# Attention on one Trainium2 core: one in three products for the row maxima is cut into pieces that fill a PSUM bank from both row halves

## The chip, the cores and the metric

The kernel runs on one core of one Trainium2 chip. The metric is the device time of one execution in microseconds (us). Before the change, three runs gave 2037.87, 2037.96 and 2039.02 us, with a median of 2037.96.

## The reference, cut to what matters

```python
def _A_ref(x, wqkv, wo):                      # B, S, D, H = 1, 2048, 640, 32
    qkv = (x @ wqkv).reshape(B, S, 3, H, Dh).transpose(2, 0, 3, 1, 4)
    q, k, v = qkv[0], qkv[1], qkv[2]          # Dh = 20
    scores = jnp.einsum("bhqd,bhkd->bhqk", q, k) * (Dh ** -0.5)
    p = _softmax(scores, axis=-1)
    o = jnp.einsum("bhqk,bhkd->bhqd", p, v)
    return o.transpose(0, 2, 1, 3).reshape(B, S, D) @ wo

def _B_ref(x, w_gate, w_up, w_down):          # F = 1728
    return (_silu(x @ w_gate) * (x @ w_up)) @ w_down

h = x + _A_ref(_layernorm(x), wqkv, wo)
h2 = h + _B_ref(_layernorm(h), w_gate, w_up, w_down)
```

The softmax needs the maximum of each row of scores. The kernel finds it in a first product of queries and keys, and computes the scores a second time, transposed, for the exponentials.

## The kernel before, in words

The program has three stages. The first, up to about 326 us, normalizes the tokens and makes queries, keys and values; a part of the row maxima is found there in the gaps (`max_four`, whose products have 256 columns, L211). The second, from 326 to about 1473 us, is the attention, and the change lies in it. The third is the feed-forward block.

The 32 heads are worked in 8 groups of 4, and the 2048 queries in 4 chunks of 512. A group and a chunk are a unit `u`; there are 32. A unit goes through 16 key tiles `kt` of 128 keys, which makes 512 key tiles in all. A head has only 20 numbers per token, so the matrices that are multiplied fill 60 or 62 rows of TensorE: two heads of a group lie in rows 0 to 63 and two in rows 64 to 127, and a product uses one of these two row halves (`b`, 0 or 1). Two products in different halves can run at the same time if they write to different PSUM banks.

In each key tile, TensorE has this to do, in the order that the string `ORDER` (L41) gives for even and odd tiles, `WsSmmSsM` and `WSsMMsSm`:

- `s` and `S` (`scores`, L1194): four score products of 512 columns, two in the first row half (`s`) and two in the second (`S`). ScalarE takes the exponential of each (L1200) into `probs`. The four write to four banks (`ps_one`) that go round, so each waits for the exponential of the tile before in the same place.
- `m` and `M` (`max_one`, L244): three products of 512 columns for the row maxima of a later unit, two in one half and one in the other, and in the next tile the other way round. VectorE reduces each to a maximum per row (L250). They use three banks (`ps_max`) that go round, so each waits for VectorE's reduction of the tile before in the same place. The two lists in `singles` hold 736 products each, 1472 in all, so they last for 490.7 key tiles.
- `W` (`weigh`, L1204): the probabilities of two tiles ago times the values. It is fp32, is done in two passes, and uses all 128 rows with four groups of 32 columns at a time. With `W` also go small steps: the end of a unit's maxima (`max_finish`), the copy of a finished output by ScalarE (`row_sums`, L1214), and preparation of the weights of the third stage by GpSimd.

When all maxima of a unit are there, `max_all` (L257) reduces the partial maxima, held in a tile `mx` per unit, over the four chunks of keys. The order of the instructions on each engine is the order of these calls; nothing is scheduled behind the author's back. An instruction that must wait for another engine waits in its engine's queue, in that order.

`clobber_nop` issues an empty instruction on VectorE, which only waits for semaphores and sets one. The first stage has 70 of them (L580): a product there is summed in one bank from both row halves, and the empty instruction stands between the halves so that they do not write to the bank at the same time.

Of the kernel before, what the change touches and what calls it, by code (L numbers as in the profile page):

```python
# [9 lines left out]
F32 = mybir.dt.float32  # L10
# [4 lines left out]
ALU = mybir.AluOpType  # L15
# [22 lines left out]
LOWEST = -3.4028234e38  # L38
GD = G * DH

ORDER = ("WsSmmSsM", "WSsMMsSm")  # L41


@with_exitstack
def tile_block(ctx: ExitStack, tc: tile.TileContext, x, wqkv, wo, wg, wu, wd, out):
# [123 lines left out]
            values[g][:, t0:t1], v_d[:, g].rearrange("(t p) w -> p t w", p=P)[:, t0:t1]  # L169
        )  # L170

    mxs = {u: stk.tile([P, 2, 2, TPC, NC], F32, name=f"mx{u}") for u in range(NU)}

    clock = dict.fromkeys(("PE", "ACT", "DVE", "POOL"), 0)
    held = [[0] for _ in range(5)]
# [64 lines left out]
    def max_one(u, kc, t, pair, b):  # L240

        ps = ps_max()
        rows = slice(b * ROW, b * ROW + NPART)
        nc.tensor.matmul(  # L244
            ps,
            queries[u][rows, pair, t * P : (t + 1) * P],
            keys[u // NC][rows, pair, kc * CH : (kc + 1) * CH],
            start=True, stop=True,
        )
        nc.vector.tensor_reduce(  # L250
            mxs[u][:, b, pair, t, kc : kc + 1], ps, axis=AX.X, op=ALU.max
        )

    def max_all(u):

        ends[u] = stk.tile([P, G * TPC], F32, name="neg", tag="neg", bufs=2)
        nc.vector.tensor_reduce(  # L257
            ends[u], mxs[u].rearrange("p b h t k -> p (b h t) k"), axis=AX.X, op=ALU.max, negate=True
        )

    def max_finish(u):
# [30 lines left out]
        if not in_projections(u, kc, t)  # L292
    ]


    evp_ctx = ExitStack()
    evp = evp_ctx.enter_context(tc.tile_pool(name="evp", bufs=2))
# [12 lines left out]
    with tc.tile_pool(name="pa", bufs=2) as pa:  # L310
# [442 lines left out]
        for c in range(NC):  # L753
            lns = []
            work = (some_keys + some_queries if c else first) + parts
            if c == NC - 1:
                work = some_keys + parts + some_queries

                es[:] = [e for e in es if e is not third]
                es.insert(1, z_tiles(NC)[0][:, :2])  # L760
            for j, (kind, *which) in enumerate(work):
                slot[0] = 18 * c + j
                while flips and not j:
                    flips.pop(0)()
                if c == 0 and j < 9:
                    for i in range(split_at[j], split_at[j + 1]):
                        split_w(i + 2)
                        if i % 2 == 1 and loaded < 8:
                            load_w(loaded)
                            loaded += 1  # L770
                if c + 1 < NC and j == 0:
                    es[:0] = [
                        t.rearrange("p k n -> p (k n)")[:, : 2 * EW].rearrange(
                            "p (i n) -> p i n", i=2
                        )
                        for t in z_tiles(c + 1)
                    ]
                    if c:
                        es[:] = es[2:] + es[:2]
                if c + 1 < NC and j == 10:  # L780
                    es[:] = [e for e in es if any(e is own for own in own_es)]
                if j == (0 if c else 3) and c + 1 < NC:
                    load_x(c + 1)
                    x_there[0] = clock["PE"] + X_LANDING
                    lns = norm(c + 1)
                if which:
                    if (c, j) == (0, 0):
                        first_blocks((0, 1), (1, 0), (1, 1), (0, 2), (1, 2))
                        for m, ps in enumerate(firsts):
                            keep(0, m, ps)  # L790
                    else:
                        (query_key if kind == "block" else value)(c, *which)
                else:
                    flip_ctx.close()
                    psum = ps_ctx.enter_context(
                        tc.tile_pool(name="psum", bufs=1, space=bass.MemoryType.PSUM)
                    )
                    turn, jobs = [0], [0]
# [51 lines left out]
    def ps_one():  # L850
# [3 lines left out]
            return psum_two.tile([P, CH], F32, name="ps_one", tag="ps_two")  # L854
        return psum.tile([P, CH], F32, name="ps_one", tag=f"ps_{(last + n - 1) % 3}")

    def ps_max():
        return psum.tile([P, CH], F32, name="ps_max", tag="ps_max", bufs=3)

    pp = att_ctx.enter_context(tc.tile_pool(name="pp", bufs=6, side="right"))  # L860
    evp_ctx.close()
# [382 lines left out]
            )  # L1244

    todo, tail, accs, closing, now = [], [], {}, {}, [0]
    singles = [[(*a, b) for a in rest] for b in range(2)]
    left = {u: sum(2 for a in rest if a[0] == u) for u in range(1, NU)}

    def next_max(b):  # L1250
        if singles[b]:
            a = singles[b].pop(0)
            max_one(*a)
            left[a[0]] -= 1
            if left[a[0]] == 0:
                max_all(a[0])
                closing[a[0]] = now[0] + 2

    def weigh_next():
        u, kt, probs = todo.pop(0)  # L1260
# [9 lines left out]
    for u in range(NU):  # L1270
# [4 lines left out]
        for kt in range(NT):  # L1275
# [626 lines left out]
```

## Time and profile before

| | |
|---|---|
| median of 3 runs | 2037.96 us |
| span of the profiled execution | 2036.6 us |
| attention with maxima, 326 to 1364 us | 1038 us |
| attention with maxima and the first output projections, 1364 to 1400 us | 36 us |
| rest of the attention, 1400 to 1473 us | 73 us |
| TensorE busy, share of the span | 99% |
| VectorE | 79% |
| ScalarE | 71% |

The profiled execution's own time is its span, from its first to its last instruction, 2036.6 us; the median of the runs is 1.4 us more. In the rows of the profile, PE is TensorE's products, PEld its weight loads, DVE VectorE, ACT ScalarE, POOL GpSimd. A row of the timeline gives the start and the length in us of one or several like instructions in a row, the line and operation, what is written and read, their number, and in brackets the idle time of the engine before. The names `ps_one` and `ps_max` tell scores and maxima apart.

### The profile page before, as it was taken

To read this page: it belongs to the slowest core of one execution; us is meant where nothing else is said; L and a number is where in the kernel's file an instruction comes from. 1 tells how busy PE (TensorE), PEld (TensorE's weight loads), DVE (VectorE), ACT (ScalarE), POOL (GpSimd) and SP (SyncE) were. 2 spreads that over 40 slices of the span, in tenths; PEclk is the share of its full clock that TensorE was granted. 3 is DMA by queue.
4 is the path that set the end of the run, shared out by engine and by line. 5 is a ranking of instruction groups with operands and counts; after the bars stand their busy time and mean duration, and the time that the engine had idled before them with its cause. 6 is when DMAs were issued, how large, how long until landed. Compare 5 with 4: busy or idle time off the path is not lost.

```text
span 2036.6 us, 40049 instructions
## 1 busy us (share of the span) xinstructions
PE 2012.6 (99%) x14322; PEld 1248.4 (61%) x14322; DVE 1608.8 (79%) x2826; ACT 1445.0 (71%) x2855; POOL 773.5 (38%) x1103
## 2 busy tenths in 40 slices
PE   8999999999999999999999999999999999999999
PEld 6999995333334333333333333345598888888888
DVE  5687778888888888888888888886378666676677
ACT  4677778999999999999999999987633222211221
POOL 6464423334342434352400011011146454754555
PEclk9999999999999999999999999999999999999999
DMA  7887563352634534435513131321158654974542
GB/s 238 262 254 261 167 206 88 115 159 80 187 104 122 168 113 146 147 129 176 156 46 79 27 92 47 92 62 55 34 182 303 221 192 157 345 273 159 202 150 94
DMA packets 194062, 310.01 MB, mean 152 GB/s; under 512 B 47760, under 2 KB 82576, under 8 KB 192840
## 3 DMA queue, kind: packets, MB, share of 16 engines
q1 hardware_dynamic: 187272, 283.85, 43.1%
q0 software_dynamic: 6496, 23.60, 3.9%
q8 instruction: 114, 1.87, 0.4%
q14 instruction: 84, 0.69, 0.1%
q10 hardware_dynamic: 96, 0.00, 0.0%
HBM read 207.75 MB, written 98.83 MB: 151 GB/s over the span
## 4 chain that ended last, share of the span: by engine, by line
PE 89%; DMA 3%; DVE 1%; ACT 1%; issue 0%; SPq 0%; POOL 0%; ACTq 0%; DVEq 0%; POOLq 0%
PE acc L1204 24%; PE ps_one L1194 16%; PE ps_a L1365 15%; PE ps_max L244 12%; PE ps_b L1459 8%; PE ps_one L575 7%; PE ps_max L211 3%; PE ps_max L925 2%; PE ps_b L925 1%; DMA halves<-j_d 1%; DMA k_stk<-k_d 0%; DMA q_stk<-q_d 0%; DMA units<-w_d 0%; ACT o L1214 0%; PE ps_max L960 0%
## 5 line engine op out<-in xcount | busy, mean ns | idle before, releaser
L1200 ACT ACTIVATE probs<-ps_one 128x512 f32<-128x512 f32 x2048 | 1056.7, 615 | 62.5 <-PE ps_one L1194 37.5
L250 DVE TENSOR_REDUCE mx<-ps_max 128x1 f32<-128x512 f32 x1472 | 926.1, 684 | 108.1 <-PE ps_one L1194 78.7
L1194 PE MATMUL ps_one<-q_stk,k_stk 62*128 62x512 f32 x2048 | 586.5, 451 | 2.7 <-DVE m L89 1.8
L1204 PE MATMUL acc<-probs,v_stk 128*32 128x512 f32 x4096 | 545.3, 605 | 0.7 <-ACT o L1214 0.6
L1194 PEld LDWEIGHTS ps_one<-q_stk,k_stk 62*128 62x128 f32 x2048 | 251.7, 184 | 433.1 <-ACT probs L1200 398.3
L244 PE MATMUL ps_max<-k_stk,q_stk 60*128 60x512 f32 x1472 | 381.4, 425 | 0.0
L244 PEld LDWEIGHTS ps_max<-k_stk,q_stk 60*128 60x128 f32 x1472 | 271.8, 186 | 23.6 <-DVE mx L250 0.9
L1580 DVE TENSOR_TENSOR tmp<-ps_a,tmp 128x512 f32<-128x512 f32 x208 | 141.2, 689 | 120.5 <-PE ps_a L1365 94.7
L233 DVE TENSOR_REDUCE mx<-ps_max 128x2 f32<-128x512 f32 x288 | 180.5, 685 | 63.6 <-PE ps_max L211 59.7
L1239 POOL TENSOR_TENSOR o<-o,rb 128x512 f32<-128x512 f32 x31 | 39.9, 1286 | 413.2 <-DMA q_stk<-q_d 235.8
L1204 PEld LDWEIGHTS acc<-probs,v_stk 128*32 128x32 f32 x4096 | 80.8, 108 | 175.6 <-issue 166.3
L223 ACT ACTIVATE ps_max<-ps_max 128x512 f32<-128x512 f32 x288 | 151.7, 584 | 46.3 <-PE ps_max L211 43.7
L1459 PE MATMUL ps_b<-halves,yp 128*128 128x320 f32 x1032 | 179.3, 309 | 1.9 <-DMA halves<-j_d 1.2
L1459 PEld LDWEIGHTS ps_b<-halves,yp 128*128 128x128 f32 x1032 | 165.2, 188 | 18.5 <-POOL yp L89 1.5
L1365 PE MATMUL ps_a<-t,units 128*128 128x512 f32 x624 | 162.6, 396 | 0.0
L1365 PE MATMUL ps_a<-z,units 128*128 128x512 f32 x516 | 133.9, 394 | 0.0
L89 POOL TENSOR_TENSOR yp<-y,yp 128x256 fp32r<-128x256 f32 x96 | 60.2, 627 | 188.3 <-ACT yp L88 180.3
L1365 PEld LDWEIGHTS ps_a<-t,units 128*128 128x128 f32 x624 | 112.6, 188 | 18.7 <-ACT tmp L1593 0.2
L1464 DVE TENSOR_TENSOR h<-ps_b,h 128x320 f32<-128x320 f32 x248 | 110.0, 481 | 6.8 <-PE ps_b L1459 5.3
L575 PE MATMUL ps_one<-z_hi,w_lo 64*128 64x512 f32 x380 | 112.6, 393 | 0.0
L575 PE MATMUL ps_one<-z_hi,w_hi 64*128 64x512 f32 x380 | 111.7, 393 | 0.0
L575 PE MATMUL ps_one<-z_lo,w_hi 64*128 64x512 f32 x380 | 111.2, 392 | 0.0
(211 smaller groups left out, 2640.3 us busy)
## 6 DMA issues: line engine op xcount, KB each, us to landing
units<-w_d SPq DMA_DIRECT2D x186, 256.0 KB
w_d<-stage SPq DMA_DIRECT2D x106, 256.0 KB
halves<-j_d SPq DMA_DIRECT2D x70, 320.0 KB
j_d<-stage SPq DMA_DIRECT2D x42, 320.0 KB
k_stk<-k_d SPq DMA_DIRECT2D x64, 160.0 KB
q_stk<-q_d SPq DMA_DIRECT2D x64, 160.0 KB
raw<-k_d SPq DMA_DIRECT2D x62, 160.0 KB
raw<-q_d SPq DMA_DIRECT2D x54, 160.0 KB
```

The lines of the kernel that those rows point to most:

```text
L223: nc.scalar.activation(ps, ps, AF.Relu)
L233: nc.vector.tensor_reduce(mx[:, b, :, t, kc], ps.rearrange("p (j n) -> p j n", j=2), axis=AX.X, op=ALU.max,)
L244: nc.tensor.matmul(ps, queries[u][rows, pair, t * P : (t + 1) * P], keys[u // NC][rows, pair, kc * CH : (kc + 1) * CH], start=True, stop=True,
L250: nc.vector.tensor_reduce(mxs[u][:, b, pair, t, kc : kc + 1], ps, axis=AX.X, op=ALU.max)
L575: nc.tensor.matmul(ps, a[rows], b[rows], start=(i == n == 0), stop=(i == 1 and n == last), skip_group_check=True,)
L1194: nc.tensor.matmul(ps, keys[u // NC][rows, p, kt * P : (kt + 1) * P], queries[u][rows, p, :], start=True, stop=True,)
L1200: nc.scalar.activation(probs[p][:, b, :], ps, AF.Exp, scale=scale)
L1204: nc.tensor.matmul(acc[32 * j : 32 * j + 32, :], values[u // NC][:, kt, j * VW : j * VW + 32], probs[j // 2][:, j % 2, :], start=(kt == 0) ...
L1365: nc.tensor.matmul(ps.rearrange("p (t n) -> p t n", t=TPC), w[k][:, i], z[k][:, :, j], start=(first and m == 0), stop=(last and m == len(n ...
L1459: nc.tensor.matmul(ps, a, b, start=(n == 0), stop=(n == len(pairs) - 1))
L1464: nc.vector.tensor_tensor(out=h, in0=ps, in1=h, op=ALU.add)
L1580: add = lambda out, ps, x: nc.vector.tensor_tensor(out=out, in0=ps, in1=x, op=ALU.add)
```

## The change

One in three of the products that were left for the attention stage (246 of 736 items of `rest`, each an item for both row halves) is done in another way. An item used to be two products of 512 columns, one in each row half, into two banks. Now it is two shared products: each takes 256 of the 512 key columns and has two pieces of 256 columns, the first from row half 0 into the left half of a bank (`x`), the second from row half 1 into the right half of the same bank (`X`). One reduction reads the whole bank and gives two maxima per row. Between the pieces stands an empty instruction on VectorE (`n`), which waits for the first piece; the second piece waits for it. Each key tile starts with `x` and has `X` as the last but one.

The order of a tile is now `WxnSmSsMXs` for all tiles: half 0 has `x`, `m` and two scores, half 1 has two scores, `M` and `X`. A tile still has three reductions. The 490 other items give 980 products of 512 columns, two in a tile; the 492 shared ones go one to a tile.

The three banks for maxima are now named one by one, and a counter (`place`) goes round over them; it is moved by one more at the start of each tile. So `x` of a tile takes the bank of the `m` of the tile before, `m` that of `M`, and `M` that of `X`.

The maxima of a unit get up to two places more (`EXTRA`). They are no longer kept in a tile per unit but in `found`, three buffers that go round; it is set up when a unit's first maximum comes, with a memset of the two extra places, and for 16 of 31 units with a copy of the maxima found in the first stage. `max_all` reduces over six places instead of four. In the first stage only the names of banks and the size of the tiles `mx` differ.

```diff
-ORDER = ("WsSmmSsM", "WSsMMsSm")
+ORDER = "WxnSmSsMXs"
+EXTRA = 2
+EVERY = 3
...
     def max_one(u, kc, t, pair, b):
...
         nc.vector.tensor_reduce(
-            mxs[u][:, b, pair, t, kc : kc + 1], ps, axis=AX.X, op=ALU.max
+            found_of(u)[:, b, pair, t, kc : kc + 1], ps, axis=AX.X, op=ALU.max
         )
+
+    found = {}
+
+    def found_of(u):
+
+        if u not in found:
+            f = found[u] = pp.tile([P, 2, 2, TPC, NC + EXTRA], F32, name="found", tag="found", bufs=3)
+            nc.vector.memset(f[:, :, :, :, NC:], LOWEST)
+            if u in mxs:
+                nc.vector.tensor_copy(f[:, :, :, :, :2], mxs.pop(u))
+        return found[u]
+
+    def max_start(u, kc, t, pair, half, column):
+
+        ps = ps_max()
+
+        def part(b):
+            rows = slice(b * ROW, b * ROW + NPART)
+            first = kc * CH + half * CH // 2
+            nc.tensor.matmul(
+                ps[:, b * CH // 2 : (b + 1) * CH // 2],
+                queries[u][rows, pair, t * P : (t + 1) * P],
+                keys[u // NC][rows, pair, first : first + CH // 2],
+                start=(b == 0), stop=True, skip_group_check=True,
+            )
+
+        def last():
+            part(1)
+            nc.vector.tensor_reduce(
+                found_of(u)[:, :, pair, t, column], ps.rearrange("p (b n) -> p b n", b=2),
+                axis=AX.X, op=ALU.max,
+            )
+
+        part(0)
+        return lambda: nc.vector.clobber_nop([nc.vector.lower_ap(ps)]), last
...
+    place = [0]
+
     def ps_max():
-        return psum.tile([P, CH], F32, name="ps_max", tag="ps_max", bufs=3)
+        place[0] += 1
+        return psum.tile([P, CH], F32, name="ps_max", tag=f"ps_max{place[0] % 3}")
...
-            order = ORDER[now[0] % 2] if singles[0] or singles[1] else "sSsSW"
+            order = ORDER if singles[0] or singles[1] or shared else "sSsSW"
+            place[0] += 1
             for op in order:
                 if op in "mM":
                     next_max(int(op == "M"))
+                elif op in "xX":
+                    next_shared(int(op == "X"))
+                elif op == "n":
+                    if begun:
+                        begun[0][1]()
```

TensorE's instructions of one key tile before the change, in their order in the program, with the engine that each waits for. `ps_one` are the scores, `ps_max` the maxima, `acc` is `W`:

```order
L1194 MATMUL ps_one_6348<-q_stk_2820,k_stk0_123 128x512 [waits Activation_49]
L1194 MATMUL ps_one_6351<-q_stk_2820,k_stk0_123 128x512 [waits Activation_49]
L244 MATMUL ps_max_6354<-k_stk0_123,q_stk_5786 128x512 [waits DVE_49]
L244 MATMUL ps_max_6357<-k_stk0_123,q_stk_5786 128x512 [waits DVE_49]
L1194 MATMUL ps_one_6360<-q_stk_2820,k_stk0_123 128x512 [waits Activation_49]
L1194 MATMUL ps_one_6363<-q_stk_2820,k_stk0_123 128x512 [waits Activation_49]
L244 MATMUL ps_max_6366<-k_stk0_123,q_stk_5786 128x512 [waits DVE_49]
L1204 MATMUL acc_6114<-probs_6303,v_stk0_124 32x512 x2
L1204 MATMUL acc_6114<-probs_6304,v_stk0_124 32x512 x2
```

The same of the changed program. `ps_max_8319` is the shared bank; its second piece waits for VectorE's sequencer, which is the empty instruction:

```order
L278 MATMUL ps_max_8319<-k_stk1_5587,q_stk_7396 128x256 [waits DVE_49]
L1250 MATMUL ps_one_8322<-q_stk_6848,k_stk1_5587 128x512 [waits Activation_49]
L250 MATMUL ps_max_8325<-k_stk1_5587,q_stk_7396 128x512 [waits DVE_49]
L1250 MATMUL ps_one_8328<-q_stk_6848,k_stk1_5587 128x512 [waits Activation_49]
L1250 MATMUL ps_one_8331<-q_stk_6848,k_stk1_5587 128x512 [waits Activation_49]
L250 MATMUL ps_max_8334<-k_stk1_5587,q_stk_7396 128x512 [waits DVE_49]
L278 MATMUL ps_max_8319<-k_stk1_5587,q_stk_7396 128x256 [waits DVE_sequencer_49]
L1250 MATMUL ps_one_8339<-q_stk_6848,k_stk1_5587 128x512 [waits Activation_49]
L1260 MATMUL acc_8311<-probs_8271,v_stk1_5588 32x512 x2
L1260 MATMUL acc_8311<-probs_8272,v_stk1_5588 32x512 x2
```

One 512-column product for maxima has become two pieces, the first at the head of the tile and the second ahead of its last score; behind `M` and its wait for VectorE, the second piece and a score are queued.

VectorE's instructions before the change around a change of unit (`mx14` is the unit's tile; L89 belongs to `max_finish`):

```order
L250 TENSOR_REDUCE mx14_139<-ps_max_11667 128x1 [waits PE_49]
L250 TENSOR_REDUCE mx14_139<-ps_max_11676 128x1 [waits PE_49]
L89 TENSOR_TENSOR m2_11694<-ps_one_11692,m2_11694 16x128 [waits DMAHW6_49,DMAHW5_49,DMAHW7_49,DMAHW0_49,Activation_49]
L250 TENSOR_REDUCE mx14_139<-ps_max_11710 128x1 [waits PE_49]
L250 TENSOR_REDUCE mx14_139<-ps_max_11713 128x1 [waits PE_49]
```

And after, where a unit's `found` is set up (the reduction of L287 is that of a shared bank; the empty instruction is not listed, its waits stand at the instruction behind it):

```order
L287 TENSOR_REDUCE found_11314<-ps_max_11650 128x2 [waits DVE_sequencer_49,PE_49]
L1281 RECIPROCAL r_11551<-r_11551 128x16 [waits DMAHW6_49,DMAHW7_49,DMAHW1_49,DMAHW0_49]
L266 MEMSET found_11696 128x16x2 [waits PE_49,DVE_sequencer_49]
L268 COPY found_11696<-mx13_133 128x16x2
L256 TENSOR_REDUCE found_11696<-ps_max_11694 128x1 [waits PE_49]
L256 TENSOR_REDUCE found_11696<-ps_max_11706 128x1 [waits PE_49]
L287 TENSOR_REDUCE found_11314<-ps_max_11688 128x2 [waits DVE_sequencer_49,PE_49]
L298 TENSOR_REDUCE neg_11711<-found_11314 128x16 [waits DVE_49]
```

The memset and the copy stand behind the empty instruction and ahead of the reduction of `m`.

More of the change, by code (lines that the diff above doesn't have):

```diff
@@ L170, in load_values @@
         )
-    mxs = {u: stk.tile([P, 2, 2, TPC, NC], F32, name=f"mx{u}") for u in range(NU)}
+    mxs = {
+        u: stk.tile([P, 2, 2, TPC, 2 if u else NC], F32, name=f"mx{u}")
+        for u in range(NU)
+        if u % NC < 2 or u == 2
+    }
     clock = dict.fromkeys(("PE", "ACT", "DVE", "POOL"), 0)
@@ L257, in max_all @@
         nc.vector.tensor_reduce(
-            ends[u], mxs[u].rearrange("p b h t k -> p (b h t) k"), axis=AX.X, op=ALU.max, negate=True
+            ends[u], (found.pop(u) if u else mxs[u]).rearrange("p b h t k -> p (b h t) k"), axis=AX.X, op=ALU.max, negate=True
         )
@@ L293, in tile_block @@
     ]
+    plain_items, shared = [], []
+    used = {}
+    for n, (u, kc, t, pair) in enumerate(rest):
+        if n % EVERY:
+            plain_items.append((u, kc, t, pair))
+        else:
+            extra = NC + used.setdefault((u, t, pair), 0)
+            used[u, t, pair] += 1
+            shared += [(u, kc, t, pair, 0, kc), (u, kc, t, pair, 1, extra)]
+    assert max(used.values()) <= EXTRA
     evp_ctx = ExitStack()
@@ L797, in tile_block @@
                     )
-                    turn, jobs = [0], [0]
+                    turn, jobs, three = [0], [0], [0]
                     def ps_one():
@@ L808, in ps_max @@
                             return psum_two.tile([P, CH], F32, name="ps_max", tag="ps_two")
-                        return psum.tile([P, CH], F32, name="ps_max", tag="ps_max", bufs=3)
+                        three[0] += 1
+                        return psum.tile([P, CH], F32, name="ps_max", tag=f"ps_max{three[0] % 3}")
                 if c == 0 and j == 6:
@@ L855, in ps_one @@
         return psum.tile([P, CH], F32, name="ps_one", tag=f"ps_{(last + n - 1) % 3}")
+    place = [0]
     def ps_max():
-        return psum.tile([P, CH], F32, name="ps_max", tag="ps_max", bufs=3)
+        place[0] += 1
+        return psum.tile([P, CH], F32, name="ps_max", tag=f"ps_max{place[0] % 3}")
     pp = att_ctx.enter_context(tc.tile_pool(name="pp", bufs=6, side="right"))
@@ L1246, in tile_block, with counted @@
     todo, tail, accs, closing, now = [], [], {}, {}, [0]
-    singles = [[(*a, b) for a in rest] for b in range(2)]
+    singles = [[(*a, b) for a in plain_items] for b in range(2)]
+    begun = []
     left = {u: sum(2 for a in rest if a[0] == u) for u in range(1, NU)}
+    def counted(u):
+        left[u] -= 1
+        if left[u] == 0:
+            max_all(u)
+            closing[u] = now[0] + 2
     def next_max(b):
@@ L1253, in next_max, with next_shared @@
             max_one(*a)
[L1254 to L1257, printed above, removed]
+            counted(a[0])
+    def next_shared(b):
+        if b == 0 and shared:
+            a = shared.pop(0)
+            begun.append((a[0], *max_start(*a)))
+        elif b == 1 and begun:
+            u, _, last = begun.pop()
+            last()
+            counted(u)
     def weigh_next():
```

## The prediction

> **What bounds the kernel now.** First I read the page's busy times and its chain of work that ended last:
>
> ```profile
> PE 2012.6 (99%) x14322; PEld 1248.4 (61%) x14322; DVE 1608.8 (79%) x2826; ACT 1445.0 (71%) x2855; POOL 773.5 (38%) x1103
> PE 89%; DMA 3%; DVE 1%; ACT 1%; issue 0%; SPq 0%; POOL 0%; ACTq 0%; DVEq 0%; POOLq 0%
> ```
>
> TensorE is never idle for long and 89% of the chain is its own. But the busy share is that of either row half, so it doesn't say how full the halves are. The stage that changes is the attention; the table of stretches and the groups within it:
>
> ```profile
> 326.00:1364.00 1038.00, 1035.59 (x7222) 409.97 (x7221) 921.25 (x1525) 1006.00 (x1982) 297.37 (x462) 1.00 0.37 111
> ...
> L1200 ACT ACTIVATE probs<-ps_one 128x512 f32<-128x512 f32 x1916 | 988.3, 614 | 31.0 <-PE ps_one L1194 6.1
> L250 DVE TENSOR_REDUCE mx<-ps_max 128x1 f32<-128x512 f32 x1436 | 903.8, 684 | 106.7 <-PE ps_one L1194 78.7 <-PE ps_max L244 24.0
> L89 DVE TENSOR_TENSOR m<-ps_one,m 16x128 fp32r<-16x128 f32 x30 | 8.4, 279 | 7.8 <-ACT m L88 7.0
> L1214 ACT ACTIVATE o<-acc 128x512 f32<-128x512 f32 x29 | 18.3, 631 | 0.7 <-DMA o_d<-o 0.7
> L1225 DVE RECIPROCAL r<-r 128x16 f32<-128x16 f32 x29 | 7.0, 243 | 0.0
> ```
>
> The 1916 exponentials are 479 key tiles in 1038.0 us, 2.17 us a tile, and the granted clock (1.00) leaves nothing to explain. ScalarE and VectorE are busy for 97% and 89% of it: little room. So one tile has to be read piece by piece. The timeline, with TensorE's, one weight load's and VectorE's rows:
>
> ```profile
> 801.82 1.89 DVE L250 TENSOR_REDUCE mx<-ps_max 128x1 f32<-128x512 f32 x3 [0.24 <-PE ps_one L1194]
> ...
> 803.16 0.50 PE L1194 MATMUL ps_one<-q_stk,k_stk 62*128 62x512 f32 x2
> 803.50 0.40 PE L244 MATMUL ps_max<-k_stk,q_stk 60*128 60x512 f32 x1
> 803.50 0.39 PE L1194 MATMUL ps_one<-q_stk,k_stk 62*128 62x512 f32 x1
> 803.74 0.52 PE L244 MATMUL ps_max<-k_stk,q_stk 60*128 60x512 f32 x2
> 803.76 0.18 PEld L244 LDWEIGHTS ps_max<-k_stk,q_stk 60*128 60x128 f32 x1
> 803.94 1.89 DVE L250 TENSOR_REDUCE mx<-ps_max 128x1 f32<-128x512 f32 x3 [0.23 <-PE ps_max L244]
> 803.97 0.40 PE L1194 MATMUL ps_one<-q_stk,k_stk 62*128 62x512 f32 x1
> 804.30 1.06 PE L1204 MATMUL acc<-probs,v_stk 128*32 128x512 f32 x8
> 805.30 0.50 PE L1194 MATMUL ps_one<-q_stk,k_stk 62*128 62x512 f32 x2
> ```
>
> One half does score 803.16, maximum 803.50, maximum 803.74, score 803.97; the other score 803.16, score 803.50, maximum 803.76, and then nothing until `W` at 804.30. So the fuller half sets the tile: 0.34 (the first product waits for its weights) + 0.24 + 0.23 + 0.33 (the last one, until `W`) + 1.00 (`W`) = 2.14 us. A 512-column product takes 0.235 of its half. The emptier half's maximum is held up by something else: VectorE's three reductions begin at 801.82 and end 1.89 later, at 803.71, and its weight load follows 0.05 after, at 803.76. That wait is hidden here, since the half has a product less to do.
>
> ScalarE in the same tile:
>
> ```profile
> 803.70 2.07 ACT L1200 ACTIVATE probs<-ps_one 128x512 f32<-128x512 f32 x4
> ```
>
> Four exponentials take 2.07 with the tail of the last; less one of 0.614, three spacings are 1.456, so ScalarE needs 0.485 each and 1.94 a tile. VectorE's spacing is (1.89 − 0.684)/2 = 0.603, so it needs 1.81 a tile.
>
> **The change part by part.** *The pieces.* How long 256 columns take shows in the first stage, where both halves run two such products each and then go on with 512 columns:
>
> ```profile
> 300.11 0.46 PE L211 MATMUL ps_max<-raw,raw 60*128 60x256 f32 x4
> 300.35 0.40 PE L575 MATMUL ps_one<-z_hi,w_lo 64*128 64x512 f32 x1
> ```
>
> Two more rows of that stage, the reductions with two outputs and the empty instructions (least, median and greatest duration in ns):
>
> ```profile
> L233 DVE TENSOR_REDUCE mx<-ps_max x288: 645/683/695, 50.0 to 321.3; 128x2 f32<-128x512 f32 x144
> L580 DVEq EVENT_SEMAPHORE  x70: 21/542/2474, 27.0 to 316.2; - x70
> ```
>
> A half runs two of them in 0.24 (300.11 to 300.35), so a piece costs 0.12, half of a whole product, and both weight loads hide. The Trainium skill ("TensorEngine Tiling (Array Packing)", Instruction Overhead) gives each matmul some 60 cycles beyond its columns. By that rule a piece would be (256+60)/(512+60) of 0.235, an estimate of 0.13, and the gain below 2 to 5 us smaller; the rows show no such cost.
>
> Each half now has three products and a piece. TensorE's own path is `x`, `m`, two scores: 0.34 − 0.115 = 0.225 until `m`, 0.235, 0.235, 0.33, and `W` 1.00: 2.025. That is 0.115 less than 2.14, the most that the change can give.
>
> *The wait that is uncovered.* `M` takes the bank of the tile before's `X`, which is reduced last, and now has `X` behind it in the same half. From the stamp of one tile's first product: `m` at 0.225; its reduction 0.44 later (803.50 to 803.94) at 0.665; the third reduction ends 1.89 later at 2.555 (a reduction with two outputs takes 683 ns by L233's row, like the others); `M`'s weight load at 2.605; its data 0.11 later at 2.715, as it must wait for these weights (the first product of a tile loses the same: 0.34 against 0.235). `X` follows at 2.95, is through 0.12 later, `W` 0.10 after that (0.33 − 0.235) at 3.17, and the next tile but one begins 1.00 later at 4.17. Two tiles in 4.17 are 2.085 a tile. This is longer than TensorE's 2.025, so VectorE's chain becomes the bound, and of the 0.115 only 2.14 − 2.085 = 0.055 remains. Queued behind `M`'s wait are `X`, a score and `W`; the score isn't due before `M`'s wait is over, `X` and `W` are late.
>
> *ScalarE's chain.* First exponential 0.54 after the stamp (803.16 to 803.70), fourth done 2.07 later at 2.61; its bank goes to the last score of the next tile, 0.05 and 0.11 later at 2.77; 0.33 to `W`, 1.00: 4.10, or 2.05 a tile. It is hidden, by 0.035 only.
>
> *The empty instruction.* `x` has streamed at 0.225 and can be seen 0.205 later (0.44 − 0.235), at 0.43. The empty instruction takes 0.02 at least by L580's row, whose median of 0.54 holds its waiting. I take 0.05. At 0.48 it is out of the way; VectorE's next reduction is due at 0.665 and `X` far later. Cost nothing, covered by 0.185 of idle time of VectorE; beyond that each 0.1 of delay costs 0.05 a tile.
>
> *Per unit.* 31 memsets and 16 copies are not in the trace of before. The nearest rows are small VectorE instructions of 0.243 (L1225) and 0.279 (L89); the lower end is nothing. They stand behind the empty instruction, so the reduction due at 0.665 starts at 0.72 after a memset alone and 0.96 with a copy: 15 × 0.055 + 16 × 0.295 = 5.5 us if each delay goes through, 0 if the other tiles absorb it; I take 4. ScalarE's copies of the output (29 of 0.631) come on top of its 1.94; it had 0.20 a tile to catch up and now has 0.145, so it is late for longer. I take 0.15 each, 4 us, between 0 and 9. `max_all` over six places and the two sequencer waits lie in VectorE's gap. The first and third stages keep their instructions; the maxima still last for some 491 tiles.
>
> **The sum.** 490 × 0.055 = 27 us, less 4 and 4, makes 19. The profiled execution's span is 2036.6 and would be 2017.6; the median of the runs is 1.4 above the span, so **2019 us**. A measurement can tell about 0.2%, 4 us, from no change. With the ends of the unit costs (0 to 15) and 0.01 a tile on the chain either way (5 us), the likeliest case alone gives 2007 to 2031.
>
> **The rivals.**
>
> *Full balance, 1990 us.* If `M`'s bank came free 0.06 earlier in each tile, TensorE's 2.025 would hold: 490 × 0.115 = 56, less 8. For it: VectorE has 0.25 of idle time a tile. Against: the weight load that follows a reduction's end by 0.05 already in this trace.
>
> *No change, 2034 to 2042.* ScalarE's chain is only 0.035 below the bound. If an exponential slips by 0.04, four of them bring it to the old time. For it: its 97% in the stage. Against: the spacing of 0.485.
>
> *Products start in order, 2046 us.* If the halves kept the program's order, the last score could not start before `X`: 2.95 + 0.33 + 1.00 = 4.28, 2.14 a tile, no gain, and 8 for the units on top. The trace speaks against it: in the tile above the second score of the emptier half starts at 803.50, and a maximum that stands ahead of it at 803.74. The Trainium skill ("TensorE: Matmul & The Clock Gate", Part 3, The mechanism) says that matmuls start and end strictly in program order; the trace disagrees.
>
> *Slower, by the empty instruction, about 2094 us.* It stands in VectorE's queue ahead of the reduction of `m`. If it passed not 0.05 but 0.54 after `x` (L580's median), it would end at 0.97 and that reduction start 0.305 late; half of this a tile is 0.15, less the 0.055, 490 × 0.0975 = 48, and 8: 56 us slower. The point from which it decides is 0.25 later than I take it. For it: all of those 0.54 could be its own. Against: the 21 ns of the fastest.
>
> **How the numbers follow.** Forecast (2007 to 2031) 0.62; full balance 0.08; no change 0.10; in order 0.06; the empty instruction 0.14. Faster by over 0.2%: 0.62 + 0.08 = 0.70; same 0.10; slower 0.06 + 0.14 = 0.20. The range from 1998 to 2048 holds the forecast, no change and in order, and a part of neither end: 0.78, with what lies between the cases about 0.8.
>
> **What would show it.** Right: a tile of about 2.08 in the attention, in one length or alternating ones that average to it; `M`'s weight load 0.05 after the end of the third reduction in most tiles, and its product of 0.50 instead of 0.39; `W` following `X`; VectorE's idle time ahead of the first reduction still near 0.25. Wrong: a tile of 2.03 with `W` following a score (full balance); exponentials with no idle time and scores that wait for them (ScalarE); last scores that never start before `X` (in order); first reductions that begin right at the end of the empty instruction, later than 0.44 after `m` (the empty instruction). Unit changes longer by over half a microsecond each would make the sum's last two terms wrong.

## The result, and the profile after

The changed kernel takes 2023.57 us (median of 4 runs, 2022.97 to 2023.85); the kernel before, on the same chip, 2038.49 (4 runs, 2037.87 to 2041.11). The ratio is 0.9927, with an interval of 0.9913 to 0.9941: 14.9 us faster, where 19 were forecast. The spans of the profiled executions, 2036.6 and 2021.5, differ by 15.1. Counted from one first product of `W` to that of a later tile, the attention divides like this:

| | before | after |
|---|---|---|
| tiles 0 to 477 (maxima, no projections) | 1034.9 us | 1016.3 us |
| of them, tiles under 2.2 us: number and mean | 406 of 2.127 us | 408 of 2.066 us |
| the longer ones: what they are over that mean, together | 18.5 us | 28.8 us |
| tiles 478 to 489 (the last with maxima) | 47.4 us | 51.2 us |
| of them, the eight with output projections, 478 to 485 | 36.2 us | 38.8 us |
| and the four behind these, 486 to 489 | 11.2 us | 12.4 us |
| the 21 tiles after these, up to the last one | 62.4 us | 62.5 us |
| from there to the end | 565.6 us | 565.2 us |

So the common tile gives 478 × 0.0605 = 28.9 us; the longer tiles take 10.3 back and tiles 478 to 489 take 3.8, which leaves 14.8.

The page, busy times and chain:

```profile
PE 1994.3 (99%) x14814; PEld 1267.7 (63%) x14814; DVE 1608.1 (80%) x2873; ACT 1434.8 (71%) x2855; POOL 773.1 (38%) x1103
PE 85%; DMA 3%; DVE 2%; issue 2%; POOL 1%; ACT 1%; SPq 1%; ACTq 0%; DVEq 0%; POOLq 0%
```

TensorE's share of the chain went from 89 to 85% and VectorE's from 1 to 2%. The sums hardly tell what happened; a pair of tiles does. Most of TensorE's products, two of its weight loads, and VectorE's reductions, in the timeline (start, length, engine, line; ps_max at L278 are the pieces, at L250 the whole products for maxima):

```profile
812.21 0.68 DVE L287 TENSOR_REDUCE found<-ps_max 128x2 f32<-128x512 f32 x1
812.47 0.38 PE L278 MATMUL ps_max<-k_stk,q_stk 60*128 60x256 f32 x1
...
812.69 0.38 PE L250 MATMUL ps_max<-k_stk,q_stk 60*128 60x512 f32 x1
812.81 0.50 PE L1250 MATMUL ps_one<-q_stk,k_stk 62*128 62x512 f32 x2
812.94 0.18 PEld L250 LDWEIGHTS ps_max<-k_stk,q_stk 60*128 60x128 f32 x1
...
813.04 0.40 PE L250 MATMUL ps_max<-k_stk,q_stk 60*128 60x512 f32 x1
...
813.11 1.29 DVE L256 TENSOR_REDUCE found<-ps_max 128x1 f32<-128x512 f32 x2 [0.23 <-PE ps_max L250]
813.15 0.39 PE L1250 MATMUL ps_one<-q_stk,k_stk 62*128 62x512 f32 x1
813.28 0.28 PE L278 MATMUL ps_max<-k_stk,q_stk 60*128 60x256 f32 x1
...
813.49 1.07 PE L1260 MATMUL acc<-probs,v_stk 128*32 128x512 f32 x8
...
814.32 0.68 DVE L287 TENSOR_REDUCE found<-ps_max 128x2 f32<-128x512 f32 x1
814.48 0.38 PE L278 MATMUL ps_max<-k_stk,q_stk 60*128 60x256 f32 x1
...
815.05 0.18 PEld L250 LDWEIGHTS ps_max<-k_stk,q_stk 60*128 60x128 f32 x1 [0.16 <-DVE found L287]
815.06 0.49 PE L250 MATMUL ps_max<-k_stk,q_stk 60*128 60x512 f32 x1
...
815.18 0.43 PE L1250 MATMUL ps_one<-q_stk,k_stk 62*128 62x512 f32 x1
815.39 0.27 PE L278 MATMUL ps_max<-k_stk,q_stk 60*128 60x256 f32 x1
...
815.59 1.06 PE L1260 MATMUL acc<-probs,v_stk 128*32 128x512 f32 x8
...
816.59 0.38 PE L278 MATMUL ps_max<-k_stk,q_stk 60*128 60x256 f32 x1
```

The first tile is 2.01 long (812.47 to 814.48), the second 2.11 (814.48 to 816.59). In both, the load of `M`'s weights waits for the shared reduction of the tile before. In the first this reduction ends at 812.89 and the load follows 0.05 after, at 812.94; that costs nothing, since the half is busy with a score until about 813.05 (812.81 + 0.235) and `M` starts at 813.04. In the second the reduction, begun at 814.32, ends at 815.00 and the load comes at 815.05, when the half has just come free; the data wait for the weights, the product shows 0.49 instead of 0.40, and `X` and `W` come after. In 382 of the 407 common tiles in which the trace shows this load, it follows the reduction's end by 0.05 to 0.07, as the prediction said it would in most; it holds up the product only in every second one. The predicted chain, step by step from the first stamp: reduction of `m` 0.665, measured 0.64; third reduction's end 2.555, measured 2.53; `M`'s load 2.605, measured 2.58; `W` 3.17, measured 3.12; the next tile but one 4.17, measured 4.12. How often this wait leaves the weight loads idle, in the waits of the stretch from 326 to 1340 us (total, times, longest):

```profile
PEld ps_max L250 <- DVE found L287: 33.0, 188, 0.3
```

188 waits of 0.18. The common tiles are of two kinds, 212 of 2.016 and 196 of 2.120 us, and in all 345 places where two common tiles follow each other there is one of each, as in the pair.

The empty instruction, with its form (least, median and greatest ns) and those who waited for it (total us, times):

```profile
L293 DVEq EVENT_SEMAPHORE  x492: 21/50/50, 322.6 to 1391.2; - x164
...
  PEld ps_max L278: 7.5, 15
  PE ps_max L278: 1.5, 5
```

It takes 50 ns. The last two rows are the weight loads and the products of the same pieces, so 15 of 492 second pieces waited for it, 7.5 us in all, and none of them in a common tile: seven (3.2 us) lie in tiles where the maxima of a unit are transposed at a change of group, and eight (4.2 us) in tiles 479 to 489, of which rows are shown under the experiments.

### The profile page after: what moved, and what is told of

Same layout as the page of the kernel before. It is cut to its first block, busy times and chain, and to the rows that moved or that the text cites. A ratio compares the mean times of both kernels' runs of the same rounds, so it can differ in the third digit from the quotient of the medians.

```text
span 2021.5 us, 42075 instructions
## 1 busy us (share of the span) xinstructions
PE 1994.3 (99%) x14814; PEld 1267.7 (63%) x14814; DVE 1608.1 (80%) x2873; ACT 1434.8 (71%) x2855; POOL 773.1 (38%) x1103
## 4 chain that ended last, share of the span: by engine, by line
PE 85%; DMA 3%; DVE 2%; issue 2%; POOL 1%; ACT 1%; SPq 1%; ACTq 0%; DVEq 0%; POOLq 0%
PE acc L1260 24%; PE ps_a L1440 15%; PE ps_one L1250 11%; PE ps_max L278 8%; PE ps_b L1534 8%; PE ps_one L627 7%; PE ps_max L250 6%; PE ps_max L217 3%; PE ps_max L981 2%; PE ps_b L981 1%; DMA halves<-j_d 1%; DVE found L256 0%; DMA w_d<-stage 0%; DMA r_d<-r 0%; PE ps_max L1016 0%
## 5 line engine op out<-in xcount | busy, mean ns | idle before, releaser
L256 DVE TENSOR_REDUCE found<-ps_max 128x1 f32<-128x512 f32 x980 | 630.5, 685 | 84.8 <-PE ps_max L250 59.8
L278 PEld LDWEIGHTS ps_max<-k_stk,q_stk 60*128 60x128 f32 x984 | 181.9, 185 | 393.8 <-DVE found L256 375.9
L250 PE MATMUL ps_max<-k_stk,q_stk 60*128 60x512 f32 x980 | 392.0, 419 | 0.2
L287 DVE TENSOR_REDUCE found<-ps_max 128x2 f32<-128x512 f32 x492 | 335.4, 682 | 1.3 <-PE ps_max L278 1.3
L278 PE MATMUL ps_max<-k_stk,q_stk 60*128 60x256 f32 x984 | 325.5, 331 | 3.2 <-DVEq L293 1.5
L1250 PEld LDWEIGHTS ps_one<-q_stk,k_stk 62*128 62x128 f32 x2048 | 303.8, 184 | 25.5 <-ACT probs L1256 20.4
L250 PEld LDWEIGHTS ps_max<-k_stk,q_stk 60*128 60x128 f32 x980 | 181.2, 185 | 49.2 <-DVE found L287 33.2
```

The costliest lines, as they stand in the source:

```text
L250: nc.tensor.matmul(ps, queries[u][rows, pair, t * P : (t + 1) * P], keys[u // NC][rows, pair, kc * CH : (kc + 1) * CH], start=True, stop=True,
L256: nc.vector.tensor_reduce(found_of(u)[:, b, pair, t, kc : kc + 1], ps, axis=AX.X, op=ALU.max)
L278: nc.tensor.matmul(ps[:, b * CH // 2 : (b + 1) * CH // 2], queries[u][rows, pair, t * P : (t + 1) * P], keys[u // NC][rows, pair, first : ...
L287: nc.vector.tensor_reduce(found_of(u)[:, :, pair, t, column], ps.rearrange("p (b n) -> p b n", b=2), axis=AX.X, op=ALU.max,)
L1250: nc.tensor.matmul(ps, keys[u // NC][rows, p, kt * P : (kt + 1) * P], queries[u][rows, p, :], start=True, stop=True,)
```

## The experiments

**Who sets the tile: reductions made shorter.** In three kernels only a part of a bank is reduced, so that maxima are missing, while TensorE's work stays.

In the kernel before (`light_before`):

```diff
-            mxs[u][:, b, pair, t, kc : kc + 1], ps, axis=AX.X, op=ALU.max
+            mxs[u][:, b, pair, t, kc : kc + 1], ps[:, : CH // 4], axis=AX.X, op=ALU.max
```

> The kernel before, but each reduction for the maxima reads only the first 128 of 512 columns (the maxima are then of a part of the keys). If the tile before was set by TensorE's fuller half, VectorE's shorter work changes nothing: 2.13 us a tile and 2033 to 2039 us in all. If VectorE's wait was part of the bound already, the tile falls by 0.05 or more and the time by 24 or more.

Measured: 2036.72 us, ratio 0.9991 (0.9982 to 1.0000), common tile 2.128. So VectorE did not set the tile before. Nor did ScalarE: the change leaves its exponentials as they were, and the tile fell below 2.127. TensorE's fuller half is left.

In the changed kernel (`light_after`), both kinds of reduction:

```diff
-            found_of(u)[:, b, pair, t, kc : kc + 1], ps, axis=AX.X, op=ALU.max
+            found_of(u)[:, b, pair, t, kc : kc + 1], ps[:, : CH // 4], axis=AX.X, op=ALU.max
...
-                found_of(u)[:, :, pair, t, column], ps.rearrange("p (b n) -> p b n", b=2),
+                found_of(u)[:, :, pair, t, column], ps.rearrange("p (b n) -> p b n", b=2)[:, :, : CH // 8],
```

> The changed kernel with reductions that read 128 columns of each bank (64 of each piece). VectorE's round of banks is then short. Theory that VectorE's round sets the changed tile (4.13 for two): what is left is TensorE's own path of 2.01 a tile, 478 x 0.055 = 26 us less than the change, about 1997. Rival that ScalarE's chain sets it: 2.05 a tile or more, 2015 to 2024. Rival that TensorE's own path is already what shows: no change, 2023.

Measured: 2008.04, ratio 0.9850 (0.9833 to 0.9866), common tile 2.040. That is between the two theories' numbers: the tile falls by 0.026 without VectorE's work, so VectorE did set it, and then stops short of 2.01. What stops it is in the timeline of this run. Each row of exponentials holds the two that touch a narrow window around the weight load of a tile's last score, which is the row behind it:

```profile
806.85 1.16 ACT L1256 ACTIVATE probs<-ps_one 128x512 f32<-128x512 f32 x2
807.52 0.18 PEld L1250 LDWEIGHTS ps_one<-q_stk,k_stk 62*128 62x128 f32 x1
...
808.86 1.22 ACT L1256 ACTIVATE probs<-ps_one 128x512 f32<-128x512 f32 x2
809.52 0.18 PEld L1250 LDWEIGHTS ps_one<-q_stk,k_stk 62*128 62x128 f32 x1
```

An exponential takes 0.614, as before the change, so the first of each two ends at 807.46 and 809.47; the loads follow 0.06 and 0.05 after. That is the chain by which the prediction gave ScalarE 2.05 a tile.

Only the shared reduction, to half of its columns (`half_read`):

```diff
-                found_of(u)[:, :, pair, t, column], ps.rearrange("p (b n) -> p b n", b=2),
+                found_of(u)[:, :, pair, t, column], ps.rearrange("p (b n) -> p b n", b=2)[:, :, : CH // 4],
```

> The changed kernel, where only the reduction of the shared bank reads less (128 of 256 columns of each piece). It is the last of a tile, and its end is what the next tile's M waits for. Theory of VectorE's round: its end comes some 0.25 sooner, two tiles would take 3.88, so TensorE's 2.01 to 2.02 is reached, about 1998 us. If VectorE's work as a whole were the bound, a third of the gain of the kernel with all reductions shortened. If ScalarE's chain is the bound: no change, 2020 to 2024.

Measured: 2011.87, ratio 0.9867 (0.9852 to 0.9881), common tile 2.042, again above the expected, for the same reason. But it has 0.024 of the 0.026 that `light_after` takes off the common tile, and 11.7 of its 15.5 us, where a third was expected if VectorE's total work were the bound: the end of the last reduction matters.

Both engines lightened (`light_both`): `light_after`, and exponentials of 448 of 512 columns with the rest set to 1, so that one in eight probabilities is not computed:

```diff
-        nc.scalar.activation(probs[p][:, b, :], ps, AF.Exp, scale=scale)
+        n = 7 * CH // 8
+        nc.scalar.activation(probs[p][:, b, :n], ps[:, :n], AF.Exp, scale=scale)
+        nc.vector.memset(probs[p][:, b, n:], 1.0)
```

> The changed kernel with VectorE's reductions cut to 128 columns, and with exponentials of 448 of 512 columns as well (VectorE sets the other 64 probabilities to 1). If the tile that is left when VectorE's work is short (2.04) is set by ScalarE's chain, from a tile's first score over four exponentials to the next tile's last score, it is now shorter by 4 x 0.06, and TensorE's own path is left: 2.01 a tile, 478 x 0.03 = 14 below the kernel with short reductions alone, about 1994 us. If something else sets the 2.04 (TensorE's queue, the empty instruction): no change, 2006 to 2010.

Measured: 1985.43, ratio 0.9735 (0.9716 to 0.9753), common tile 2.015; the longer tiles fell too, from 27.4 us over the mean in `light_after` to 19.5, which the expectation had not counted. Most of that is in the 22 first tiles of a unit that are not at a change of group; they stand behind ScalarE's copy of an output: 0.34 over the mean in `light_after`, 0.06 here. Four exponentials now take 1.85 instead of 2.07 and have idle time ahead of them:

```profile
813.15 1.85 ACT L1257 ACTIVATE probs<-ps_one 128x448 f32<-128x448 f32 x4 [0.16 <-PE ps_one L1250]
```

So the changed kernel has three bounds close above each other: TensorE 2.015, ScalarE 2.040, VectorE through the banks 2.066.

**The order of a tile.** The last score ahead of `X`, though still behind `M` (`score_first`):

```diff
-ORDER = "WxnSmSsMXs"
+ORDER = "WxnSmSsMsX"
```

> The changed kernel with the last score ahead of the second piece in the program's order. If the row halves run independently, the order of these two means nothing: 2023 us, within 2. If products started in program order, the last score would no longer stand behind the piece that waits for M: up to 0.1 a tile, 1980 to 2005.

Measured: 2023.84, ratio 0.9927 (0.9912 to 0.9942), common tile 2.066. The place makes no difference, so the last score does not stand behind the start of `X` in the other row half. In the timeline above, of the kernel with `X` ahead of that score, the last scores start at 813.15 and 815.18 and `X` at 813.28 and 815.39. The Trainium skill ("TensorE: Matmul & The Clock Gate", Part 3, The mechanism) has matmuls start and end strictly in program order; this run and these four starts disagree. In both cases `M`'s wait for VectorE was over; a product that still waits for another engine holds up what is queued behind it, as `empty_later` below shows.

The counter not moved at the start of a tile (`no_shift`), so that each product waits for the reduction in the same place of the tile before, and `x`, not `M`, for the shared one:

```diff
-            place[0] += 1
             for op in order:
```

> The changed kernel without the additional step of the bank counter at each tile: each product takes the bank that it had in the tile before. Then x, the first of a tile, waits for the reduction that ends last, 2.555 after the stamp of the tile before, and 0.05 more: a tile of 2.60, 2.60 - 2.07 = 0.53 more than with the step, 478 x 0.53 = 255, about 2280 us. If the banks' order doesn't matter: 2023.

Measured: 2257.21 in one run, common tile 2.59; `x` now starts half a microsecond late in every tile and everything follows it. The expected 2.60 came out of the same arithmetic as the change's 2.085. The time is 23 below the expected 2280, mostly since the longer tiles are only some 6 us over the mean and not 28.8.

The empty instruction behind VectorE's first reduction (`empty_later`):

```diff
-ORDER = "WxnSmSsMXs"
+ORDER = "WxSmnSsMXs"
```

> The changed kernel with the empty instruction behind the reduction of m in VectorE's queue instead of ahead of it. It then waits for m's product too (seen at 0.66 after the stamp), passes at 0.71, and TensorE's queue lets X and the last score go at 0.76; the score's data start 0.11 later at 0.87 instead of 0.69, W at 1.20: a tile of 2.20, 478 x 0.13 = 62 more, about 2086 us. If the place of the empty instruction costs nothing: 2023.

Measured: 2068.96 in one run, common tile 2.192. The time is lower than expected since the longer tiles are only some 11 us over the mean. The second piece now waits for the empty instruction in 481 of 492 cases:

```profile
812.53 1.29 DVE L256 TENSOR_REDUCE found<-ps_max 128x1 f32<-128x512 f32 x2 [0.31 <-PE ps_max L250]
812.65 0.18 PEld L278 LDWEIGHTS ps_max<-k_stk,q_stk 60*128 60x128 f32 x1 [0.19 <-DVEq L293]
```

`X`'s weights come 0.12 after the start of the reduction behind which the empty instruction stands, not after its end: it does not wait for the reduction to be done, but it does wait for it to start. And the last score, in the other half but queued behind `X`, now waits with it: the two loads lie 0.003 apart in the median tile, while in the change the score's load comes 0.05 ahead of `X`'s. That is why the tile grows.

**What takes the gain back.** The old products and order with the new books: `found`, memset, copy, six places (`books_only`):

```diff
-ORDER = "WxnSmSsMXs"
+ORDER = ("WsSmmSsM", "WSsMMsSm")
...
-        if n % EVERY:
+        if True:
             plain_items.append((u, kc, t, pair))
...
-            order = ORDER if singles[0] or singles[1] or shared else "sSsSW"
-            place[0] += 1
+            order = ORDER[now[0] % 2] if singles[0] or singles[1] or shared else "sSsSW"
```

> The old products and the old order, with only the bookkeeping of the change: maxima in the three round buffers, memset and copy at each unit, six places in the last reduction. In the old tile VectorE's chain has room, so this costs 0 to 2 us: 2038 to 2040. If these instructions stop TensorE by themselves, their full time of 31 x 0.085 + 16 x 0.175 = 5.4 us shows: 2044.

Measured: 2039.60 against 2037.99, ratio 1.0008 (0.9999 to 1.0017). The books alone cost 1.6 us, hardly more than can be told from nothing.

`found` set up after a tile's operations and not among them (`found_ahead`):

```diff
             for op in order:
...
+            if singles[0]:
+                found_of(singles[0][0][0])
+            if shared:
+                found_of(shared[0][0])
```

> The changed kernel, with a unit's buffer set up at the end of the tile before its first maximum, so that memset and copy lie in VectorE's gap ahead of the empty instruction. If they delayed the first reduction (0.06 with a memset, 0.2 to 0.3 with a copy): up to 4 us less than the change, 2020 to 2023. If the next tiles absorb that delay: 2023 to 2024.

Measured: 2024.38, ratio 0.9920 (0.9907 to 0.9934); the longer tiles are 27.9 us over the mean instead of 28.8. Moving the memset and the copy brings nothing that can be told; single profiled executions differ by more in their longer tiles (in that of `extra_first` below, tiles 0 to 475, which its edit leaves alone, take 3.3 us more than in the change).

The second of each three items shared, not the first (`share_second`). In the change, three tiles take 2.78 to 3.14 us, each with the first scores of a unit. The timeline of after, in one of them:

```profile
695.07 0.18 PEld L278 LDWEIGHTS ps_max<-k_stk,q_stk 60*128 60x128 f32 x1 [0.84 <-DVE found L256]
...
696.17 0.47 PE L1250 MATMUL ps_one<-q_stk,k_stk 62*128 62x512 f32 x1 [0.72 <-DMA q_stk<-m]
```

The scores wait for the transfer that puts the unit's maxima into the query rows. In every fourth unit the last item was shared, and a shared product is the last in a tile, so the maxima close a tile later: the long tile with their transpose is now the 44th of 64, and was the 43rd.

```diff
-        if n % EVERY:
+        if n % EVERY != 1:
```

> The changed kernel, but of each three items the second is shared instead of the first. The last item of every fourth unit is then not a shared one, and its maxima are complete one key tile sooner, as in the kernel before. If the three tiles of 2.8 to 3.1 us (where scores wait for the DMA that brings the maxima into the queries' rows) come from that one tile, they go: 2 to 3 us less than the change, 2021. If they come from something else: 2023 to 2024.

Measured: 2023.03, ratio 0.9919 (0.9905 to 0.9932). The transpose is back in the 43rd tile and the three tiles have 2.12 to 2.13. The last unit's maxima end a tile sooner too, and tiles 486 to 489 take 11.5 us instead of 12.4. In time this can't be told from the change.

The tiles with projections. These eight took 4.53 each before and now 4.59 to 4.65 and 5.07 to 5.11 in turn, 2.6 us more together. The timeline of after, in two of them:

```profile
1355.93 0.49 DVE L987 TENSOR_TENSOR h<-ps_max,h 128x320 f32<-128x320 f32 x1 [2.01 <-PE ps_max L981]
1356.48 0.18 PEld L250 LDWEIGHTS ps_max<-k_stk,q_stk 60*128 60x128 f32 x1 [0.24 <-DVE h L987]
...
1361.58 0.21 DVE L990 BATCH_NORM_AGGREGATE mvs<-st 128x2 f32<-128x12 f32 x1
1361.69 0.18 PEld L278 LDWEIGHTS ps_max<-k_stk,q_stk 60*128 60x128 f32 x1 [0.44 <-DVEq L293]
```

Two waits are read there: `M` has the bank of the projection in the same tile and waits for VectorE's sum (L987); and in every second tile the empty instruction stands in VectorE's queue behind the normalization's aggregate, and the second piece is 0.44 late.

The four tiles behind them have no projections, yet take 1.2 us more. Of these, 0.9 came back in `share_second`. In the first three of the four, other steps of the normalization stand ahead of the empty instruction, and the second pieces' weights wait 0.59, 0.55 and 1.11 us. The third of these waits:

```profile
1389.24 0.61 DVE L1004 TENSOR_SCALAR z<-h,mvs,r_c 128x640 f32<-128x640 f32 x1
1389.38 0.18 PEld L278 LDWEIGHTS ps_max<-k_stk,q_stk 60*128 60x128 f32 x1 [1.11 <-DVEq L293]
```

`extra_first` puts the projection ahead of `W` and so ahead of `x`:

```diff
                 else:
+                    if extra:
+                        extra.pop(0)()
                     if len(todo) == 2:
                         weigh_next()
                     for v in ready:
                         max_finish(v)
-                    if extra:
-                        extra.pop(0)()
```

> The changed kernel, where the steps of the output projection stand ahead of W instead of behind it. In the 12 tiles that have maxima and projections, the empty instruction stood behind VectorE's statistics, which wait for VectorE's own sums, and X came late (tiles of 4.6 and 5.1 instead of 4.53). With W's 1.0 us in between, they should fall to about 4.5: 3 us less than the change, 2020 to 2021. If it is the banks that the projections take out of turn: no change, 2023 to 2024.

Measured: 2028.34, ratio 0.9935 (0.9922 to 0.9949), no gain. The tiles with maxima and projections are eight, not the 12 of the expectation. They have 4.79 to 4.86 now, about the mean of the two lengths in the change and 0.4 us less together, since the projection comes right behind `X` and waits for its own bank:

```profile
1356.67 1.29 DVE L256 TENSOR_REDUCE found<-ps_max 128x1 f32<-128x512 f32 x2 [0.28 <-PE ps_max L250]
1357.41 0.74 PEld L981 LDWEIGHTS ps_max<-wo_hi,o_hi 128*128 128x128 f32 x5 [0.65 <-DVE found L256]
```

So a wait was exchanged for another; that the two named above are the whole cause of the 2.6 us is read from the trace and was not shown by taking them away.

The three repairs together (`all_three`: `share_second`, `extra_first` and `found_ahead`):

> The three edits together: second item shared, projections ahead of W, buffers set up a tile ahead. If each acts at its own places, the sum of what they give one by one, 5 to 8 us less than the change: 2016 to 2019.

Measured: 2021.18, ratio 0.9907 (0.9894 to 0.9921), less than expected and not apart from the change's 0.9913 to 0.9941. No version that computes everything is shown to beat the change.

## Why the prediction was right, and where it was off

**The bound before** was TensorE's fuller half: right. `light_before` took VectorE's work away and left the tile as it was, and the unchanged exponentials ran in a shorter tile after the change.

**The uncovered wait** was right in mechanism and nearly in size: 4.12 for two tiles instead of 4.17, a tile of 2.066 instead of 2.085. `half_read` shortened only the reduction that ends the chain and brought nearly all that could be had; `no_shift` moved the wait to another product and came out at the predicted length. Of the 0.115 that the change could give, half was lost to this wait.

**ScalarE's chain**, 2.05 and hidden by 0.035: measured 2.040, seen as soon as VectorE's was gone. **TensorE's own path**, 2.025: 2.015 once both were light. By the 60 cycles that the Trainium skill ("TensorEngine Tiling (Array Packing)", Instruction Overhead) gives each matmul beyond its columns, a piece would take (256 + 60)/(512 + 60) of a product and the path some 0.01 more than 2.025, an estimate; the measured value lies below 2.025, so no run shows that cost.

**The empty instruction** costs nothing in a common tile: right. It takes 50 ns, the value that was assumed. The prediction looked at common tiles alone, and the 15 waits lie in the others. `empty_later` shows the rival's mechanism was real, and that 0.2 us later in VectorE's queue it decides.

**In order** is refuted by `score_first` and the starts in the timeline; **full balance** by the common tile; **no change** did not happen, though the margin to ScalarE is small.

**Per unit**, 8 forecast and 10.3 measured, but made up otherwise, so that the sum came near is in part luck:

- ScalarE's copies of the output: the 22 tiles that show them are 0.31 over the mean where they were 0.15 over, 3.5 us; forecast 4. That ScalarE's lateness is the cause is shown by `light_both`, where shorter exponentials bring 0.34 down to 0.06, while shorter reductions alone (`light_after`) do not.
- The memset and the copy: forecast 4. They take 85 and 233 ns in the mean (rows below; the copy has a median of 175). `found_ahead` finds nothing to be had from moving them, and with all the books they cost 1.6 us in the old order (`books_only`): nearer to the lower end of the bound, 0, than to the 4 that was taken.
- Three scores that wait for a transfer, 2.8 us over the mean: no term of the sum. The prediction had asked what is late behind `M` in a tile and not when a unit's last maximum is done.
- The 23 tiles with a transpose that lie within a group had 2.37 to 2.39, and 19 of them still have 2.37 to 2.41, so they have not gained the 0.06: together they are 1.9 us further over the mean than before. The sum gave the gain to all tiles.
- The other 2.1 us are spread over more of the longer tiles; their cause stays open.

The groups of after, with the number, busy time in us and mean in ns:

```profile
L268 DVE COPY found<-mx 128x32 f32<-128x32 f32 x16 | 3.7, 233 | 0.2 <-PE ps_one L1250 0.2
L266 DVE MEMSET found<- 128x32 f32 x31 | 2.6, 85 | 3.6 <-PE ps_one L1250 2.9
```

**The last tiles with maxima** are the term that was missing. The sum took 0.055 for all of 490 tiles. Eight of them hold the projections as well, which write to the same three banks and put work on VectorE's queue ahead of the empty instruction; they lost 2.6 us. The four behind them lost 1.2, of which 0.9 hangs on the last unit's maxima that end a tile later (`share_second`). The larger gain of the common tile (28.9 against 27) about makes up for the larger unit costs, so the 4 us between 19 and 14.9 are about the 3.8 of these twelve tiles.

## What to carry to other kernels

When work is evened out between two units that run side by side, the emptier one's waits lose their cover: write down each chain that goes round (bank, reduction, bank again; bank, exponential, bank again) over as many tiles as it takes to close, and take the longest, not the work of each unit. Then list the tiles that are not like the others, since each has other neighbours in the queues and in the buffers that go round. An instruction that only passes on a semaphore costs what stands ahead of it in its queue, so its place counts more than its length.

## What the runs showed of the hardware that was not expected

- Tiles of one and the same program took 2.02 and 2.12 in turn in the mean, and only the sum over two is set by the chain. A mean over a window hides which wait is at work.
- The product that waits for the empty instruction gets its weights 0.12 after the reduction ahead of that instruction has begun (`empty_later`), without waiting for its end.
- A reduction takes some 0.14 us and 0.27 for each 256 columns: 0.68 for 512 columns above, and in the timelines of `half_read` and `light_both` 0.42 for 256 and 0.28 for 128. The one of `half_read`:

```profile
812.78 0.42 DVE L287 TENSOR_REDUCE found<-ps_max 128x2 f32<-128x256 f32 x1
```

And the one of `light_both`:

```profile
813.81 0.28 DVE L287 TENSOR_REDUCE found<-ps_max 128x2 f32<-128x128 f32 x1
```
